# A preset of partial maxima moves from GpSimd to VectorE, in 27 of 32 units

## The chip, the cores and the metric

The kernel runs on one core of one Trainium2 chip. The metric is the time of one execution on the device, in microseconds (us); lower is better. Engines are named as the profile names them: PE is TensorE (PEld its weight loads), DVE is VectorE, ACT is ScalarE, POOL is GpSimd, SP is SyncE, which issues nearly all DMAs here.

## The reference

One transformer block over 2048 tokens of width 512: attention with 32 query heads of width 16 that share one key and one value head, then a gated MLP of width 1792, both behind a layer norm and a residual. All in float32.

```
q = (ln(x) @ wq) as 32 heads of 16;  k = ln(x) @ wk;  v = ln(x) @ wv
p = softmax((q @ k.T) * 16 ** -0.5)           # over all 2048 keys
h = x + concat(p @ v) @ wo
gate = ln(h) @ W_gate;  up = ln(h) @ W_up
out = h + (gate * (gate > 0) * up) @ W_down
```

## The kernel before

**Units.** Attention is done in 32 units. A unit is 256 tokens of 8 heads, that is 2048 query rows. Each unit passes twice over the keys. The first pass finds each query row's greatest score (letters `m` and `M` of the row of letters below, lower and upper half of PE's rows): a matmul of 128 query rows by 512 keys into one PSUM bank (line 655), and a `tensor_reduce` of DVE that leaves one number per row (line 665). The second pass (`e`, `E`) makes the scores again with keys on the partitions (line 702), ACT takes the exponential (line 705), and a value block (`O`, line 718) multiplies with v.

**The partial maxima.** A unit's numbers go to a tile `mpart`, `[128, 2, 2, 4, 4]`: half of PE's rows, part, block of 128 rows, and last the slot j, one for each 512 keys. When all are there, `max_finish` reduces over the four slots (line 670) and three more DVE operations and a DMA round trip bring the maximum into the queries of the second pass. Two tiles `mpart` take turns (`bufs=2`).

**Joint maxima.** In places the third and fourth blocks of keys are done together (letters `d`, `D`): PE multiplies with `kdiff`, the difference of the two blocks' keys; ACT makes its positive part (line 659); and DVE adds it to the fourth block's scores and takes the maximum in one operation (line 662, with an accumulator read behind it). The result stands in slot 3, and slot 2 is never written. So that line 670 can read it, the whole tile is set to -3e38 when the unit begins, by a POOL `memset` on line 651.

**What else POOL does.** The MLP's weights come by DMA as raw float32 (`wraw`) and are split into a rounded and a rest part, two POOL operations a tile (lines 246 and 247), the same for the hidden activations `hT`. For each of 14 hidden blocks f of a token tile POOL runs, in this order: the product `hf` (line 913), the split of two tiles `gu` (gate and up weights of f+2), of `hT`, and of `wd`. It also normalises the attention output (line 768: `raw` times `scale`, which come by DMA) and splits it. POOL works through its queue in order of the program.

**What sets the order.** A row of letters `ORDER` is written in the kernel; a loop takes a letter after another and emits that pass on PE at once, with what ACT and DVE do with its result. MLP passes are the letters `g`, `G` (line 304). Work of POOL and the DMAs is emitted when a simple model of the clocks of the engines (`on`, `at`, `due`) says so; the model has no entry for the memset. Each engine then runs its own instructions in the order of emission, and semaphores hold an instruction until its operands are ready and its buffer is free.

Of the kernel before, what the change touches and what calls it, by code (L numbers as in the profile page):

```python
# [26 lines left out]
STEPS = NB * 2  # L27
# [10 lines left out]
PASS, LOAD, SEEN, CHANGE, VALUE, BACK, TURN = 230, 107, 425, 95, 882, 237, 214  # L38

EXP, EXP_FREE, RED, RED_FREE, COPY, ADD, FREE = 494, 650, 600, 740, 541, 600, 150  # L40
JOINT, APART, RELUS = 640, 2900, 3
ROUND, DIFF, PRODUCT, SCALE, HOP, ISSUE = 640, 1290, 1150, 640, 2600, 600
APPLY, LANDING, ASKED, SPREAD, RAW_LAG = 705, 4700, 5500, 5600, 1500

# [113 lines left out]
def block_kernel(ctx: ExitStack, tc: tile.TileContext, x, wq, wkv, wo, wgu, wd, out):  # L158
    nc = tc.nc
# [37 lines left out]
    def bank(tag=None):  # L197
        if tag is None:
            tag = rota["tags"][rota["n"] % len(rota["tags"])]
            rota["n"] += 1  # L200
        return ps.tile([128, 512], F32, name=tag, bufs=1)
# [7 lines left out]
    def on(engine, t, ns):  # L209

        clk[engine] = max(clk[engine], t) + ns
        return clk[engine]
# [418 lines left out]
    mpart = {}  # L631

    def max_step(m):

        i = m % STEPS
        if i < STEPS // 2:
            return i // 8, i // 4 % 2, i % 4
        return 2 + i % 2, (i - STEPS // 2) // 8, (i - STEPS // 2) // 2 % 4
# [1 line left out]
    def key_of(m):  # L640
        return "key", max_step(m)[0]

    relus = {}

    def max_mm(m, ab, tag, apart=False):

        v = m // STEPS
        j, p, c = max_step(m)
        if v not in mpart:
            mpart[v] = sb.tile([128, 2, 2, 4, 4], F32, name="mpart", bufs=2)  # L650
            nc.gpsimd.memset(mpart[v], -3e38)
        r = slice(64 * ab, 64 * ab + 62)
        b = bank(tag)
        keys = kdiff[r] if apart else kaug[r, j * 512:(j + 1) * 512]
        nc.tensor.matmul(b, qaug[v][r, p, c * 128:(c + 1) * 128], keys, start=True, stop=True)  # L655
        part = mpart[v][:, ab, p, c, j:j + 1]
        if apart:
            relus[ab] = sb.tile([128, T], F32, name="relu", bufs=RELUS)
            nc.scalar.activation(relus[ab], b, AF.Relu)  # L659
        elif ab in relus:  # L660
            over = relus.pop(ab)
            nc.vector.tensor_tensor_reduce(out=over, in0=b, in1=over, scale=1.0, scalar=-3e38, op0=ALU.add, op1=ALU.max,  # L662
                                           accum_out=part)
        else:
            nc.vector.tensor_reduce(part, b, axis=AX.X, op=ALU.max)  # L665
# [552 lines left out]
    while not done():  # L1218
# [78 lines left out]
        letter = next(order)  # L1297
# [8 lines left out]
        kind, k = letter.upper(), int(letter.isupper())  # L1306
# [4 lines left out]
        if kind == "O":  # L1311
            value_block(on_)
            v, i = divmod(on_, NB)
# [12 lines left out]
        elif kind == "E":  # L1326
# [7 lines left out]
            ge[k] += 1  # L1334
        elif kind == "D":
            max_mm(me[k], k, tag, True)
            lanes[k] = s + PASS
            slots[k] = len(joined)
# [6 lines left out]
        elif kind == "M":  # L1345
            joint = k in relus
            max_mm(me[k], k, tag)
            lanes[k] = s + PASS
            r0 = max(clk["V"], s + SEEN, relu_end.pop(k, 0.0))
# [61 lines left out]
```

## Time and profile before

| | |
|---|---|
| median of 3 runs | 1771.95 us (1770.25 to 1772.96) |
| the profiled execution | 1770.07 us |
| its span, first to last instruction | 1768.3 us |
| mean granted TensorE clock | 0.981 |
| busy: PE, DVE, ACT, POOL | 1707.0, 1388.4, 1299.8, 844.4 us |

The profiled execution has 1.8 us around its span. In the answers quoted below, a row of the chain or the timeline reads: start, duration, engine, line, operation, out <- in, count, and in brackets how long the engine sat idle before it and what ended that. A row of the waits reads: who, on which line <- for whom: total us, times, longest. A row of a table of stretches gives the busy time of each engine with the number of its instructions, then the granted TensorE clock (1.00 is full speed), the DMAs' share and rate.

### The profile page before, as it was taken

How to read it: one execution, taken by the hardware profiler on the slowest of the kernel's cores; microseconds unless marked ns; L12 is line 12 of the kernel's file. 1: busy time of each engine (PE TensorE's matmuls, PEld its weight loads, DVE VectorE, ACT ScalarE, POOL GpSimd, SP SyncE). 2: the span in 40 equal slices, each digit the busy share in tenths (PEclk: the TensorE clock that was granted, in tenths of full speed). 3: DMA queues.
4: the chain of work that ended last, by engine and by line, in shares of the span. 5: the costliest groups of instructions: out<-in, count | busy, mean ns of one | idle time of the engine just before them, and what ended most of it. 6: DMA issues, size and time to landing. Idle time of an engine off the chain costs nothing.

```text
span 1768.3 us, 40468 instructions
## 1 busy us (share of the span) xinstructions
PE 1707.0 (97%) x15566; PEld 1153.7 (65%) x15566; DVE 1388.4 (79%) x2546; ACT 1299.8 (74%) x2628; POOL 844.4 (48%) x1034
## 2 busy tenths in 40 slices
PE   8999999889999999999899989999999999999999
PEld 6774345556666676676667667666656667666688
DVE  8698998768888887878688768877769888894355
ACT  6577998668778777877677767875667877778734
POOL 4624001545626456376635547276443766454510
PEclk9899999989999999999999999999999999999999
DMA  3233011221223222233213222222222222233333
GB/s 127 72 110 112 23 32 41 80 73 62 82 70 98 65 89 89 77 95 94 64 47 104 77 76 88 69 84 67 79 81 65 86 85 76 62 107 98 112 124 118
DMA packets 101972, 144.09 MB, mean 81 GB/s; under 512 B 27156, under 2 KB 39572, under 8 KB 101780
## 3 DMA queue, kind: packets, MB, share of 16 engines
q1 hardware_dynamic: 100724, 141.19, 25.9%
q8 instruction: 122, 2.00, 0.5%
q14 instruction: 70, 0.57, 0.1%
q10 hardware_dynamic: 1056, 0.33, 0.1%
HBM read 119.73 MB, written 21.49 MB: 80 GB/s over the span
## 4 chain that ended last, share of the span: by engine, by line
PE 77%; POOL 12%; issue 6%; DVE 2%; DMA 1%; ACT 1%; SPq 0%; POOLq 0%; ACTq 0%; DVEq 0%
PE B L304 24%; PE O L718 23%; PE B L702 15%; PE B L655 11%; POOL gu L247 4%; PE B L295 3%; POOL wd L247 2%; POOL gu L246 2%; DVE mpart L665 1%; POOL hT L247 1%; POOL hf L913 1%; POOL wd L246 1%; PE B L536 1%; POOL hT L246 1%; PE O L970 0%
## 5 line engine op out<-in xcount | busy, mean ns | idle before, releaser
L705 ACT ACTIVATE p<-B 128x512 f32<-128x512 f32 x2048 | 1067.8, 613 | 337.8 <-PE B L655 193.5
L665 DVE TENSOR_REDUCE mpart<-B 128x1 f32<-128x512 f32 x1760 | 1101.1, 683 | 251.1 <-PE B L655 150.0
L655 PE MATMUL B<-kaug,qaug 62*128 62x512 f32 x1904 | 714.7, 422 | 28.8 <-DVE mpart L665 23.9
L702 PE MATMUL B<-qaug,kaug 64*128 64x512 f32 x2048 | 712.0, 414 | 20.2 <-DVE mpart L665 19.4
L304 PE MATMUL B<-hn,gu 64*128 64x256 f32 x4704 | 569.2, 281 | 0.0
L304 PEld LDWEIGHTS B<-hn,gu 64*128 64x128 f32 x4704 | 545.0, 186 | 22.2 <-issue 15.4
L718 PE MATMUL O<-p,vv 128*32 128x512 f32 x4096 | 511.0, 607 | 0.0
L702 PEld LDWEIGHTS B<-qaug,kaug 64*128 64x128 f32 x2048 | 342.4, 186 | 217.8 <-DVE mpart L665 69.0
L655 PEld LDWEIGHTS B<-kaug,qaug 62*128 62x128 f32 x1904 | 333.8, 186 | 89.0 <-DVE mpart L665 37.4
L304 PE MATMUL B<-wd,hT 64*128 64x512 f32 x1176 | 295.4, 402 | 0.1
L913 POOL TENSOR_TENSOR hf<-hf,ga 128x256 f32<-128x256 f32 x88 | 64.6, 734 | 421.3 <-ACT hf L911 400.3
L247 POOL TENSOR_TENSOR gu<-wraw,gu 128x512 fp32r<-128x512 f32 x191 | 247.7, 1297 | 15.9
L718 PEld LDWEIGHTS O<-p,vv 128*32 128x32 f32 x4096 | 103.0, 109 | 213.4 <-issue 195.7
L304 PEld LDWEIGHTS B<-wd,hT 64*128 64x128 f32 x1176 | 196.9, 189 | 23.8 <-issue 10.2
L246 POOL TENSOR_SCALAR gu<-wraw 128x512 fp32r<-128x512 f32 x191 | 118.4, 620 | 25.3 <-PE B L304 24.8
L247 POOL TENSOR_TENSOR wd<-wraw,wd 128x512 fp32r<-128x512 f32 x90 | 115.8, 1287 | 7.5
L662 DVE CUSTOM_DVE_ANT_0 relu<-B,relu 128x512 f32<-128x512 f32 x144 | 96.7, 685 | 21.4 <-PE B L655 7.3
L768 POOL TENSOR_TENSOR raw<-raw,scale 128x512 f32<-128x512 f32 x15 | 19.3, 1287 | 192.3 <-DMA scale<-r_dram 126.0
L659 ACT ACTIVATE relu<-B 128x512 f32<-128x512 f32 x144 | 84.8, 605 | 23.9 <-PE B L655 23.2
L304 PE MATMUL B<-wo,act 64*128 64x512 f32 x384 | 88.5, 391 | 0.0
L247 POOL TENSOR_TENSOR hT<-hf,hT 128x256 fp32r<-128x256 f32 x97 | 74.1, 764 | 8.1
L905 ACT ACTIVATE ga<-B 128x256 f32<-128x256 f32 x112 | 44.1, 393 | 37.1 <-PE B L295 22.7
(156 smaller groups left out, 1112.2 us busy)
## 6 DMA issues: line engine op xcount, KB each, us to landing
wraw<-wgu SPq DMA_DIRECT2D x224, 256.0 KB
wraw<-wd SPq DMA_DIRECT2D x112, 256.0 KB
q_dram<-act SPq DMA_DIRECT2D x32, 256.0 KB
qaug<-q_dram SPq DMA_DIRECT2D x62, 128.0 KB
o_dram<-osb SPq DMA_DIRECT2D x31, 256.0 KB
x<-x SPq DMA_DIRECT2D x18, 256.0 KB
out<-h SPq DMA_DIRECT2D x16, 256.0 KB
qaug<-q_dram SPq DMA_DIRECT2D x62, 64.0 KB
```

The costliest lines, as they stand in the source:

```text
L246: nc.gpsimd.tensor_scalar(dst[:, 0], src, 1.0, 0.0, op0=ALU.mult, op1=ALU.add)
L247: nc.gpsimd.tensor_tensor(dst[:, 1], src, dst[:, 0].bitcast(F32), op=ALU.subtract)
L295: nc.tensor.matmul(out(self.bank), l(a), r(b), start=i == 0, stop=i == len(self.ops) - 1)
L304: mm = nc.tensor.matmul(out(self.bank), l(a)[rows], r(b)[rows], start=opens and which == 0, stop=closes and which == 1)
L655: nc.tensor.matmul(b, qaug[v][r, p, c * 128:(c + 1) * 128], keys, start=True, stop=True)
L659: nc.scalar.activation(relus[ab], b, AF.Relu)
L662: nc.vector.tensor_tensor_reduce(out=over, in0=b, in1=over, scale=1.0, scalar=-3e38, op0=ALU.add, op1=ALU.max, accum_out=part)
L665: nc.vector.tensor_reduce(part, b, axis=AX.X, op=ALU.max)
L702: nc.tensor.matmul(b, kaug[r, kb * 128:(kb + 1) * 128], qaug[v][r, p, :], start=True, stop=True)
L705: nc.scalar.activation(probs[g][:, ab], b, AF.Exp, scale=DH ** -0.5)
L718: nc.tensor.matmul(obank[v][32 * h:32 * h + 32], vv[:, kb, :], probs[g + p][:, ab], start=kb == 0, stop=kb == NB - 1)
L913: nc.gpsimd.tensor_tensor(hf[:, :n], hf[:, :n], ga[:, :n], op=ALU.mult)
```

## The change

The preset of a unit's whole `mpart` tile (64 numbers a partition) on POOL is gone. Ahead of the loop, the kernel counts through the row of letters which units have joint maxima: 27 of the 32. In these alone DVE presets slot 2, which is 16 numbers a partition, `memset` on what is line 658 of the changed kernel. In the other five units all four slots are written, and nothing is preset. `CLEAR` is the cost that the clock model takes for the DVE operation, and it is 0. The row of letters is the same, and the lines behind the change have numbers 8 higher.

```diff
-JOINT, APART, RELUS = 640, 2900, 3
+JOINT, APART, RELUS, CLEAR = 640, 2900, 3, 0
...
-    relus = {}
+    relus, joint_units, counts = {}, set(), [0, 0]
+    for letter in ORDER:
+        if letter in "mMdD":
+            k = int(letter.isupper())
+            if letter in "dD":
+                joint_units.add(counts[k] // STEPS)
+            counts[k] += 1
...
     def max_mm(m, ab, tag, apart=False):
...
             mpart[v] = sb.tile([128, 2, 2, 4, 4], F32, name="mpart", bufs=2)
-            nc.gpsimd.memset(mpart[v], -3e38)
+            if v in joint_units:
+                nc.vector.memset(mpart[v][:, :, :, :, 2:3], -3e38)
+                on("V", 0.0, CLEAR)
```

Leaving out the presets, the order of instructions on PE, DVE, ACT, POOL and SP is the same in both kernels. Two places show the move, both at the begin of the eighth unit (342 us in the trace). First POOL's queue in the kernel before; `hf` is the product of one hidden block, `gu`, `hT` and `wd` are the tiles that POOL splits behind it:

```order
L913 TENSOR_TENSOR hf_4648<-hf_4648,ga_4647 128x256
L246 TENSOR_SCALAR gu_4652<-wraw_4492 128x512
L247 TENSOR_TENSOR gu_4652<-wraw_4492,gu_4652 128x512
L246 TENSOR_SCALAR gu_4655<-wraw_4494 128x512
L247 TENSOR_TENSOR gu_4655<-wraw_4494,gu_4655 128x512
L246 TENSOR_SCALAR hT_4378<-hf_4648 128x256
L247 TENSOR_TENSOR hT_4378<-hf_4648,hT_4378 128x256
L246 TENSOR_SCALAR wd_4660<-wraw_4382 128x512
L247 TENSOR_TENSOR wd_4660<-wraw_4382,wd_4660 128x512
L651 MEMSET mpart_4673 128x64
L913 TENSOR_TENSOR hf_4803<-hf_4803,ga_4802 128x256
```

The memset of the new unit's `mpart` stands behind a hidden block's nine operations, the first of which needs ACT's result; in the changed kernel POOL goes from `wd` to the next `hf`.

Second DVE's queue at the same place, in the kernel before (`ISA` rows are the joint maxima of line 662 and their accumulator reads; `mpart_4045` is the unit that is ending, `mpart_4673` the one that begins):

```order
L662 ISA relu_4579,mpart_4045<-B4_4638,relu_4579 128x512
L662 ISA mpart_4045 128x1
L662 ISA relu_4633,mpart_4045<-B5_4666,relu_4633 128x512
L662 ISA mpart_4045 128x1
L665 TENSOR_REDUCE mpart_4673<-B0_4675 128x1
L665 TENSOR_REDUCE mpart_4673<-B4_4691 128x1
L665 TENSOR_REDUCE mpart_4673<-B3_4694 128x1
```

And in the changed kernel (the tiles' running numbers are 3 lower):

```order
L670 ISA relu_4576,mpart_4042<-B4_4635,relu_4576 128x512
L670 ISA mpart_4042 128x1
L670 ISA relu_4630,mpart_4042<-B5_4663,relu_4630 128x512
L670 ISA mpart_4042 128x1
L658 MEMSET mpart_4670 128x16
L673 TENSOR_REDUCE mpart_4670<-B0_4672 128x1
L673 TENSOR_REDUCE mpart_4670<-B4_4688 128x1
L673 TENSOR_REDUCE mpart_4670<-B3_4691 128x1
```

The preset now stands on DVE right ahead of the unit's first reduce, which before was on another engine than its preset and waited for a semaphore of POOL's besides the one of PE's; of the reduces only the first of a unit did so.

## The prediction

> **What bounds the kernel now.** I read the page's busy times first, then the waits by engine, then the preset's own line, then the timeline and a table of stretches at the places that these named.
>
> ```profile
> PE 1707.0 (97%) x15566; PEld 1153.7 (65%) x15566; DVE 1388.4 (79%) x2546; ACT 1299.8 (74%) x2628; POOL 844.4 (48%) x1034
> ...
> DVE mpart L665 <- POOL mpart L651: 49.8, 10, 8.6
> ...
> PE B L655 <- DVE mpart L665: 23.9, 7, 7.1
> PE B L702 <- DVE mpart L665: 19.4, 4, 7.0
> ...
> L651 POOL MEMSET mpart<- x32: 141/152/161, 25.2 to 1543.3; 128x64 f32 x32
> ```
>
> PE is the bound: it idles 1768.3 - 1707.0 = 61 us in all, and in 23.9 + 19.4 = 43.3 us of them it waited for a reduce of DVE. DVE in turn waited 49.8 us for the memset, which itself lasts 0.15 us. The timeline shows how so short an operation costs so much:
>
> ```profile
> 334.33 0.73 POOL L913 TENSOR_TENSOR hf<-hf,ga 128x256 f32<-128x256 f32 x1 [0.89 <-ACT hf L911]
> 334.54 0.08 DVE L662 DVE_READ_ACCUMULATOR2_ANT mpart<- 128x1 f32 x1
> 335.50 0.39 PE L655 MATMUL B<-kaug,qaug 62*128 62x512 f32 x1
> 341.97 0.15 POOL L651 MEMSET mpart<- 128x64 f32 x1
> 342.15 1.89 DVE L665 TENSOR_REDUCE mpart<-B 128x1 f32<-128x512 f32 x3 [7.53 <-POOL mpart L651]
> 342.90 0.79 PE L702 MATMUL B<-qaug,kaug 64*128 64x512 f32 x1 [7.01 <-DVE mpart L665]
> ```
>
> The memset stood in POOL's queue behind a hidden block (hf, gu, hT, wd) that POOL began at 334.33 and that took 7.6 us. DVE stops at 334.6 at the new unit's first reduce, the banks fill, PE stops at 335.9. All go on when the memset is done: DVE 0.03 us after it, PE 0.75 us later, after one reduce. So a head-of-line wait on POOL stops the bound, at 342 us for 7.01 us. Seven more places have it:
>
> ```profile
> 160.59 1.29 DVE L665 TENSOR_REDUCE mpart<-B 128x1 f32<-128x512 f32 x2 [2.98 <-POOL mpart L651]
> 388.67 0.69 DVE L665 TENSOR_REDUCE mpart<-B 128x1 f32<-128x512 f32 x1 [7.83 <-POOL mpart L651]
> 884.51 1.29 DVE L665 TENSOR_REDUCE mpart<-B 128x1 f32<-128x512 f32 x2 [8.49 <-POOL mpart L651]
> 1041.55 1.89 DVE L665 TENSOR_REDUCE mpart<-B 128x1 f32<-128x512 f32 x3 [8.55 <-POOL mpart L651]
> 1195.97 2.73 DVE L665 TENSOR_REDUCE mpart<-B 128x1 f32<-128x512 f32 x4 [4.31 <-POOL mpart L651]
> 1250.06 1.29 DVE L665 TENSOR_REDUCE mpart<-B 128x1 f32<-128x512 f32 x2 [3.76 <-POOL mpart L651]
> 1305.95 1.29 DVE L665 TENSOR_REDUCE mpart<-B 128x1 f32<-128x512 f32 x2 [5.14 <-POOL mpart L651]
> ```
>
> The eight are 48.6 of the 49.8 us. The next table is the one on which the sum rests. Each of its first eight stretches runs from PE's stop to the end of the low clock that follows:
>
> ```profile
> 159.67:165.85 6.18, 4.51 (x21) 1.48 (x25) 4.58 (x9) 2.97 (x6) 0.89 (x2) 0.72 0.09 23
> 335.89:346.75 10.86, 3.85 (x17) 1.65 (x19) 2.93 (x6) 1.59 (x4) 5.98 (x8) 0.69 0.18 48
> 382.31:394.54 12.23, 5.12 (x27) 1.28 (x26) 3.26 (x7) 0.63 (x2) 6.08 (x8) 0.58 0.17 49
> 878.58:889.47 10.89, 4.22 (x21) 4.12 (x22) 4.03 (x7) 2.42 (x5) 5.64 (x8) 0.69 0.05 14
> 1036.16:1046.49 10.33, 4.20 (x20) 3.73 (x21) 4.56 (x11) 2.39 (x4) 5.10 (x8) 0.67 0.03 5
> 1191.51:1200.09 8.58, 3.38 (x16) 2.03 (x19) 3.96 (x8) 1.26 (x3) 4.26 (x6) 0.80 0.01 2
> 1247.51:1254.70 7.19, 3.90 (x21) 1.57 (x24) 4.38 (x8) 0.70 (x2) 2.43 (x4) 0.76 0.08 17
> 1302.33:1312.73 10.40, 6.03 (x31) 2.47 (x34) 4.71 (x11) 2.08 (x5) 3.42 (x6) 0.67 0.14 38
> sum 76.66, PE 35.22 PEld 18.34 DVE 32.41 ACT 14.04 POOL 33.80; mean PE 4.40 PEld 2.29 DVE 4.05 ACT 1.75 POOL 4.23
> ...
> 339.93:346.75 6.82, 3.85 (x17) 1.65 (x19) 2.93 (x6) 0.94 (x2) 2.10 (x4) 0.50 0.13 38
> 400.00:860.00 460.00, 459.90 (x4482) 311.75 (x4480) 383.78 (x706) 359.80 (x730) 263.57 (x322) 1.00 0.26 80
> ```
>
> Length less PE's busy time is the idle time: 76.66 - 35.22 = 41.4 us. But the stop costs more than its idle time. From 339.93 to 346.75 the granted clock is 0.50, and PE worked 3.85 us of it, all after the stop. All eight stretches contain such a spell (their mean clock is 0.58 to 0.80), and in 460 us without a stop the clock is 1.00. In that long stretch an instruction of PE's takes 460 / 4482 = 0.1026 us; the eight hold 174 instructions, which at that pace take 17.9 us, not 35.2.
>
> **The rule on the clock.** The Trainium skill, "TensorE: Matmul & The Clock Gate", Part 1, says that TensorE falls to half clock after an idle window of about 3.4 us and comes back after as much work. The six stops of 4.4 us and more agree; the ones of 1.67 us (first row) and 3.29 us (seventh) are followed by half clock too, which is sooner than the rule. By that page's price, half of the throttled time is lost: some 17 of the 35.2 us on top of the idle time, an estimate by which the kernel would come out 3 us faster than by my sum.
>
> **The removed memset.** What do the eight stretches take without the wait? At least PE's time at full clock, the count by 0.1026 us. And at least DVE's, which works at its own clock, less the lead that DVE has because it stopped earlier than PE: its wait, less PE's idle time, plus the 0.75 us between their restarts. Row by row (lead; DVE's work less lead; PE's time):
> - 2.06; 2.52; 2.15
> - 1.27; 1.66; 1.74
> - 1.47; 1.79; 2.77
> - 2.57; 1.46; 2.15
> - 3.17; 1.39; 2.05
> - -0.14; 4.10; 1.64
> - 1.22; 3.16; 2.15
> - 1.52; 3.19; 3.18
>
> The greater of the last two, summed, is 21.7 us, so 76.7 - 21.7 = 55.0 us come back. The two smaller DVE waits (49.8 - 48.6 = 1.2 us) I count as 0.8, since PE has 43.3 - 41.4 = 1.9 us of idle time for DVE elsewhere. Sum: 55.8. Ends: 41.4 if only the idle time returned, and 76.7 - 17.9 + 1.2 = 60.0 if PE alone set the pace. I stand nearer the upper, since both engines' work is counted. POOL's own 32 x 0.15 = 4.8 us count nothing: POOL is busy 48% of the time and waits elsewhere.
>
> **The new memset on DVE.** 27 instructions on 16 numbers a partition. The rows nearest are
>
> ```profile
> L187 DVE MEMSET vv<- 128x16 f32 x1 | 0.1, 72 | 0.1
> L674 DVE CAST msplit<-mfin x32: 174/175/1297, 85.7 to 1597.2; 128x16 fp32r<-128x16 f32 x32
> L674 DVE CAST msplit<-mfin 128x16 fp32r<-128x16 f32 x32 | 10.9, 341 | 1.1
> ```
>
> The first has the operation and the size: 27 x 0.072 = 1.9 us. The cast has the size and is held at times (0.175 us in the median, 1.297 at most); priced like its mean, 27 x 0.341 = 9.2 us. The lower end is 0, where DVE was idle at a unit's begin anyway. A gain is excluded, as DVE only gets work. I take 1.9 and put all of it on the path, because DVE is what PE waits for at these places. It waits for no other engine's tile: the one that read the buffer last is DVE itself (line 670), earlier in its queue. Behind it on DVE stands the unit's first reduce, and behind that PE's banks.
>
> The Trainium skill, "SBUF — State Buffer", section "Who interferes with whom", says that a cast can take the port pair that DVE shares with GpSimd, and that a DVE instruction with at most one SBUF input outside the two-port modes doesn't contend. By it the memset isn't held and the sum is that of 0.072; the spread of the cast agrees with the page's first half, and no row shows a memset beside a busy POOL.
>
> **What is late next.** In the stop POOL and the DMAs went on while PE did not; now PE comes up to 9 us earlier to the same place. POOL then had time to spare: its idle time up to its next operation covers the shift unless it is shorter. The shortest are
>
> ```profile
> 350.94 0.74 POOL L913 TENSOR_TENSOR hf<-hf,ga 128x256 f32<-128x256 f32 x1 [8.82 <-ACT hf L911]
> 892.31 1.28 POOL L768 TENSOR_TENSOR raw<-raw,scale 128x512 f32<-128x512 f32 x1 [7.83 <-DMA scale<-r_dram]
> 1209.84 1.29 POOL L768 TENSOR_TENSOR raw<-raw,scale 128x512 f32<-128x512 f32 x1 [13.90 <-DMA scale<-r_dram]
> 1315.09 1.29 POOL L768 TENSOR_TENSOR raw<-raw,scale 128x512 f32<-128x512 f32 x1 [9.17 <-DMA scale<-r_dram]
> ...
> 1200.66 0.24 DVE L752 RECIPROCAL sums<-sums 128x16 f32<-128x16 f32 x1
> ```
>
> The shifts there are 10.86 - 1.74 = 9.1, 10.89 - 2.15 = 8.7, 8.58 - 4.10 = 4.5 and 10.40 - 3.19 = 7.2 us, so POOL comes 0.3 and 0.9 us too late at the first two. I count 1.2 us. At the other two the DMAs bring the reciprocals of line 752, which stood on DVE behind the stopped reduce (at 1200.66 in one case) and so move with it.
>
> **Sum.** 55.8 - 1.9 - 1.2 = 52.7 us. The profiled execution, 1770.07 us, becomes 1717.4; against the median of 1771.95 that is 1719 us, 3.0% less. About 0.2%, 3.5 us, is what a measurement can tell from no change.
>
> **Rivals.**
> - *Only the idle time returns*: DVE and ACT, freed of their rest, set the pace where PE had crawled. 1771.95 - 41.4 - 0.8 + 3.1 = 1733. For it, DVE is busy 79%; against it, its work in the stretches is counted above. Chance 0.12.
> - *POOL becomes the wait*: PE comes to the weights before POOL has split them. The block that begins at 334.33 runs to 342 whatever DVE does. The last three stretches, where raw or a late DMA stands first in POOL's queue, would lose their 4.5 + 4.0 + 7.2 = 15.7 us: 1735. Against it, the idle times above, and no row of the waits of PE names gu or wd. Chance 0.10.
> - *The wait was another's*: the semaphore named came last only by chance, and PE stays stopped. Then 1774. Against it, DVE restarts within 0.03 us of the memset's end. Chance 0.02.
> - *Slower: the new memset is held on DVE.* It stands ahead of every reduce of its unit, so a hold stops PE as the old one did. To eat 55 us each of the 27 must be held 2.0 us; the longest hold of a like operation is the cast's 1.297 us, and even that every time leaves 1771.95 - 55.8 + 35 = 1751. Over 1776 only with holds beyond any row. Chance 0.02.
>
> My forecast (1713 to 1727) has 0.71; the last 0.03 is for other ends, such as a new stop elsewhere. The range goes from 1711 (upper end 60.0, next to nothing paid) to 1734, which takes in the first rival and part of the second. Faster by over 0.2%: 0.95; within: 0.03; slower: 0.02.
>
> **What would show it.** Right: DVE's waits have no row for POOL at mpart; PE's waits for line 665's successor (673) fall from 43 to a few us; no spell of 0.50 between 160 and 1700 us; memsets of DVE at some 70 ns; mean clock from 0.981 to 0.99 or more; PE's instruction count unchanged. Wrong: PE or PEld waiting for gu or wd for several us, spells of 0.50 that remain, memsets of several hundred ns, or DVE's waits for ACT or PE grown at the unit begins.

## The result, and the profile after

The changed kernel takes 1713.66 us (median of 4 runs, 1712.52 to 1715.31) where the kernel before takes 1772.45 on the same chip: 58.8 us less, a ratio of 0.967 with a 95% interval of 0.9653 to 0.9686. The forecast was 1719 (1711 to 1734). The profiled execution has a span of 1710.8 us against 1768.3, which is 57.5 us less, and a mean clock of 0.993 against 0.981.

The busy times on the page, and of the chain of waits the shares by engine (before, PE had 77% of that chain and POOL 12%):

```profile
PE 1691.1 (99%) x15566; PEld 1148.1 (67%) x15566; DVE 1388.6 (81%) x2573; ACT 1298.6 (76%) x2628; POOL 841.6 (49%) x1002
...
PE 95%; DVE 2%; POOL 1%; issue 1%; DMA 0%; ACT 0%; POOLq 0%; SPq 0%; DVEq 0%; ACTq 0%
```

PE has the same 15566 instructions. Its idle time fell from 61.3 us to 1710.8 - 1691.1 = 19.7, by 41.6 us, and its busy time from 1707.0 to 1691.1, by 15.9 us. The two make up the 57.5 us: the first is the stops, the second is low clock, since the same instructions took less time.

The waits by engine, PE's on DVE and DVE's longest:

```profile
PE B L710 <- DVE mpart L673: 1.1, 2, 0.8
PE B L663 <- DVE mpart L673: 0.2, 1, 0.2
...
DVE mpart L673 <- PE B L663: 144.8, 159, 3.8
```

PE's 43.3 us of waits for the reduces are 1.3 us, and DVE's waits have no row for the preset. The preset's own line, and the timeline of DVE, POOL and ACT at the place that stood at 342 us before:

```profile
L658 DVE MEMSET mpart<- x27: 72/72/72, 26.2 to 1498.6; 128x16 f32 x27
...
333.07 0.08 DVE L670 DVE_READ_ACCUMULATOR2_ANT mpart<- 128x1 f32 x1
333.10 0.67 DVE L673 TENSOR_REDUCE mpart<-B 128x1 f32<-128x512 f32 x1
333.12 0.07 DVE L658 MEMSET mpart<- 128x16 f32 x1
334.03 1.29 DVE L673 TENSOR_REDUCE mpart<-B 128x1 f32<-128x512 f32 x2 [0.26 <-PE B L663]
...
339.40 1.29 POOL L247 TENSOR_TENSOR wd<-wraw,wd 128x512 fp32r<-128x512 f32 x1
340.00 0.38 ACT L919 ACTIVATE hf<-B 128x256 f32<-128x256 f32 x1
340.64 0.74 POOL L921 TENSOR_TENSOR hf<-hf,ga 128x256 f32<-128x256 f32 x1
```

In DVE's queue the memset stands ahead of the unit's first reduce, which is the one at 333.10; the record of the memset begins 0.02 us behind that of the reduce and ends inside it. Ahead of the second reduce DVE is idle for 0.26 us, because of a matmul; before, it was idle for 7.53 us ahead of the first. POOL splits the same block as before, until 340.7, and PE does not wait for it. POOL has no idle time left ahead of the next `hf`: ACT's part of it ends at 340.38 and POOL takes it up at 340.64, 0.3 us late.

The eight stretches of the prediction, found again in the changed kernel by their matmuls (the n-th of each kind), and taken from the start of the last matmul ahead of the stop to the first matmul that starts behind the low clock. Before, these took 6.6, 11.4, 13.1, 11.4, 10.9, 9.1, 7.8 and 11.1 us, 81.4 in all:

```profile
161.75:164.66 2.91, 2.91 (x24) 0.99 (x24) 2.36 (x5) 2.33 (x5) 1.57 (x2) 1.00 0.11 24
334.03:336.15 2.12, 2.12 (x20) 0.91 (x18) 2.12 (x5) 1.71 (x4) 2.03 (x3) 1.00 0.02 9
...
1152.42:1155.78 3.36, 2.56 (x18) 1.16 (x19) 3.33 (x8) 1.65 (x3) 3.19 (x5) 1.00 0.10 30
1202.80:1205.36 2.56, 2.56 (x24) 1.22 (x24) 2.56 (x6) 1.10 (x3) 2.39 (x4) 1.00 0.03 10
...
sum 22.60, PE 21.80 PEld 11.26 DVE 20.84 ACT 14.10 POOL 20.34; mean PE 2.72 PEld 1.41 DVE 2.61 ACT 1.76 POOL 2.54
```

All have clock 1.00, and 81.4 - 22.6 = 58.8 us came back.

### The profile page after: what moved, and what is told of

Same layout as the page of the kernel before. It is cut to its first block, busy times and chain, and to the rows that moved or that the text cites. A ratio compares the mean times of both kernels' runs of the same rounds, so it can differ in the third digit from the quotient of the medians.

```text
span 1710.8 us, 40447 instructions
## 1 busy us (share of the span) xinstructions
PE 1691.1 (99%) x15566; PEld 1148.1 (67%) x15566; DVE 1388.6 (81%) x2573; ACT 1298.6 (76%) x2628; POOL 841.6 (49%) x1002
## 4 chain that ended last, share of the span: by engine, by line
PE 95%; DVE 2%; POOL 1%; issue 1%; DMA 0%; ACT 0%; POOLq 0%; SPq 0%; DVEq 0%; ACTq 0%
PE B L304 29%; PE O L726 28%; PE B L710 18%; PE B L663 14%; PE B L295 4%; DVE mpart L673 1%; PE B L536 1%; PE O L978 0%; PE B L411 0%; POOL kaug L517 0%; PE B L603 0%; DVE kaug L517 0%; PE B L1053 0%; DVE msplit L682 0%; DMA qaug<-c_dram 0%
## 5 line engine op out<-in xcount | busy, mean ns | idle before, releaser
L304 PEld LDWEIGHTS B<-hn,gu 64*128 64x128 f32 x4704 | 544.2, 186 | 22.5 <-issue 15.4
L726 PE MATMUL O<-p,vv 128*32 128x512 f32 x4096 | 504.1, 600 | 0.0
L663 PEld LDWEIGHTS B<-kaug,qaug 62*128 62x128 f32 x1904 | 332.1, 185 | 62.1 <-ACT p L713 18.4
L304 PE MATMUL B<-wd,hT 64*128 64x512 f32 x1176 | 288.7, 395 | 0.1
L247 POOL TENSOR_TENSOR gu<-wraw,gu 128x512 fp32r<-128x512 f32 x191 | 247.9, 1298 | 15.9
L304 PEld LDWEIGHTS B<-wd,hT 64*128 64x128 f32 x1176 | 193.3, 185 | 23.7 <-issue 10.2
```

The source lines that it names most:

```text
L247: nc.gpsimd.tensor_tensor(dst[:, 1], src, dst[:, 0].bitcast(F32), op=ALU.subtract)
L304: mm = nc.tensor.matmul(out(self.bank), l(a)[rows], r(b)[rows], start=opens and which == 0, stop=closes and which == 1)
L726: nc.tensor.matmul(obank[v][32 * h:32 * h + 32], vv[:, kb, :], probs[g + p][:, ab], start=kb == 0, stop=kb == NB - 1)
```

## The experiments

Two questions were open behind a result that agreed: which part of the change takes the stops away, since it does three things at once (another engine, a smaller region, fewer units); and which terms of the sum were off by 6 us. All ran beside runs of the kernel before, whose medians lie between 1772.2 and 1772.6 us; times are medians. The edits are shown against the changed kernel, that of part 1 against the kernel before.

**The base.** The changed kernel again, on the chip of three of the kernels below: the one with the preset earlier on POOL, the one with eight memsets for one, and the one with none.

> The changed kernel once more, as the base on this chip for the three beside it. Every theory: 1713.7 us, give or take 1.5, some 58.8 us under the kernel before.

1714.72 us, ratio 0.9674 (0.9658 to 0.9689).

**Part 1: the place in POOL's queue.** The preset stays on POOL, whole tile, all units, and is emitted earlier.

```diff
+    def preset(v):
+        mpart[v] = sb.tile([128, 2, 2, 4, 4], F32, name="mpart", bufs=2)
+        nc.gpsimd.memset(mpart[v], -3e38)
...
         if v not in mpart:
-            mpart[v] = sb.tile([128, 2, 2, 4, 4], F32, name="mpart", bufs=2)
-            nc.gpsimd.memset(mpart[v], -3e38)
+            preset(v)
...
     def max_finish(v):
...
         at(t + HOP, landed)
+        if v + 2 < len(UNITS):
+            at(t, lambda: v + 2 in mpart or preset(v + 2))
```

> The preset stays on POOL, whole tiles in all 32 units, but is emitted when the tile's last reader (two units back) has finished, about one unit ahead of its use. Theory (the place in POOL's queue made the stops): the stops go as with VectorE, 1713 to 1717 us, no low clock between 160 and 1700 us, and DVE waits under 3 us for the memset in all. Rival (the engine matters: a semaphore from POOL or POOL's work at the unit begins costs the time wherever the memset stands): it stays above 1750 us.

1715.15 us, ratio 0.9677 (0.966 to 0.9694): the same as the changed kernel. DVE's waits have no row for the memset. The wait for a free tile went to POOL, where it costs nothing (waits of POOL):

```profile
POOL mpart L648 <- DVE mfin L674: 85.5, 12, 44.7
```

So for a preset of the whole tile it was the place. POOL may preset the tile, even wait 44.7 us for it, if nobody is behind it at that moment. One spell of low clock stands between 160 and 1700 us against the expectation, at 1648 us. The changed kernel that ran beside it has one at 1646 (in both the mean clock from 1600 to 1700 us is 0.98), so it is not this preset's.

**Part 2: the smaller region and fewer units, on POOL.**

```diff
             if v in joint_units:
-                nc.vector.memset(mpart[v][:, :, :, :, 2:3], -3e38)
-                on("V", 0.0, CLEAR)
+                nc.gpsimd.memset(mpart[v][:, :, :, :, 2:3], -3e38)
```

> One part of the change alone: the preset of slot 2 in the 27 joint units, on POOL as before; the five other units have none. Theory (the place in POOL's queue makes the stops): only the stop at 160 us goes, which is that of a unit without joint maxima, so 3 to 4 us under the kernel before, about 1768.5. Rival (the preset of 64 numbers or its number of instructions matters): more than 10 us under it.

1713.78 us, ratio 0.9671 (0.9656 to 0.9685). My expectation, 1768.5, missed by 55 us: here the memset stands in POOL's queue exactly where it stood before, behind the same blocks, and no stop is left. DVE's waits for POOL, all of them:

```profile
DVE hf L915 <- POOL gu L247: 11.2, 2, 6.5
DVE hf L915 <- POOL gu L246: 3.5, 1, 3.5
DVE xn L385 <- POOL rs L364: 0.8, 1, 0.8
```

None is for the preset. In the program, a unit's first reduce writes slot 0. The whole preset writes it too, so that reduce had to wait for POOL; a preset of slot 2 alone concerns only reduces into slot 2 and the final one. The timeline shows it at the begin of the eighth unit, whose first reduce is the one at 335.67:

```profile
335.67 0.69 DVE L672 TENSOR_REDUCE mpart<-B 128x1 f32<-128x512 f32 x1
336.62 1.29 DVE L672 TENSOR_REDUCE mpart<-B 128x1 f32<-128x512 f32 x2 [0.27 <-PE B L662]
...
343.26 0.14 POOL L658 MEMSET mpart<- 128x16 f32 x1
```

The reduces run while POOL is still 7.6 us away from the memset of their tile. The next reduce that has a wait for POOL's semaphore starts at 374.99, when the memset is long done.

**Part 3: fewer units alone**, the whole tile on POOL in 27 units, to tell the region from the five dropped presets.

```diff
             if v in joint_units:
-                nc.vector.memset(mpart[v][:, :, :, :, 2:3], -3e38)
-                on("V", 0.0, CLEAR)
+                nc.gpsimd.memset(mpart[v], -3e38)
```

> The preset on POOL in the 27 joint units alone, but of the whole tile, where the kernel with the preset of slot 2 alone on POOL came out at 1713.8 us. Theory (what holds DVE is that the preset writes slot 0, which the unit's first reduce writes too; a preset of slot 2 alone holds only a reduce into slot 2, dozens of DVE's instructions later): the stops come back at seven places, all but that at 160 us, 1767 to 1770 us. Rival (dropping the preset in the five other units shifted POOL's queue enough): within 5 us of 1713.8.

1769.1 us, ratio 0.9979 (0.9969 to 0.9988). The stops are back, all but that at 160 us:

```profile
DVE mpart L672 <- POOL mpart L658: 46.7, 8, 8.6
```

So in part 2 it was the region, not the count.

**Part 4: the engine alone**, whole tile on DVE in all 32 units.

```diff
-            if v in joint_units:
-                nc.vector.memset(mpart[v][:, :, :, :, 2:3], -3e38)
-                on("V", 0.0, CLEAR)
+            nc.vector.memset(mpart[v], -3e38)
```

> The other part of the change alone: the preset moves to VectorE, of the whole tile and in all 32 units (128x64, some 0.112 us each by the two that another kernel ran at its start). Theory (either part by itself takes the stops away, and VectorE hides 0.1 us at a unit's begin): 1713 to 1717 us. Rival (only with the narrow preset do the stops go): above 1760. If VectorE hides nothing: 32 x 0.112 - 27 x 0.072 = 1.6 us over the changed kernel, 1716.

1719.58 us, ratio 0.9685 (0.9662 to 0.9707), runs from 1713.35 to 1721.03. No stops: moving the preset is enough for that too. But the median lies 2.6 us above the 1717 that I gave as the upper end and 5.9 above the changed kernel. The runs spread widely and the intervals of the two overlap; the traces say more. Matched matmul by matmul with the changed kernel's, this kernel's lie 3.3 us later at 200 us and 7.4 later at 1600, so it lost 4.1 us over 28 presets. The three kernels without a preset on DVE (those of parts 1 and 2, and the last one below) lost 0.8 to 1.2 us in the same stretch, so about 1 us is what this comparison can tell. DVE at the begin of the eighth unit:

```profile
336.86 0.09 DVE L668 DVE_READ_ACCUMULATOR2_ANT mpart<- 128x1 f32 x1
336.91 0.11 DVE L657 MEMSET mpart<- 128x64 f32 x1
337.12 1.97 DVE L671 TENSOR_REDUCE mpart<-B 128x1 f32<-128x512 f32 x3
```

The first reduce starts 0.26 us behind the accumulator read, where in the changed kernel it is 0.02 (333.07 and 333.10). The whole preset writes slot 0, so the reduce has to wait for it on DVE too; its record has a wait for DVE's own semaphore. So the narrow region is worth some 3 to 4 us on this engine.

**The memset's price.** Eight memsets for one, and none.

```diff
             if v in joint_units:
-                nc.vector.memset(mpart[v][:, :, :, :, 2:3], -3e38)
-                on("V", 0.0, CLEAR)
+                for _ in range(8):
+                    nc.vector.memset(mpart[v][:, :, :, :, 2:3], -3e38)
```

> Each of the 27 presets on VectorE is done eight times instead of once: 189 more memsets of 0.072 us, 13.6 us more work for DVE. Theory of the prediction (DVE's added time at the unit begins lies on PE's path): 13 to 14 us over the changed kernel, about 1727. Rival (DVE has slack at most unit begins, so that the 1.9 us of the prediction were not paid): under 5 us over it, below 1719.

1737.24 us, ratio 0.9802 (0.9788 to 0.9817): 22.5 us over the base, more than the 13.6 of either theory. The group of its memsets shows why:

```profile
L659 DVE MEMSET mpart<- 128x16 f32 x216 | 15.6, 72 | 13.3
```

Memsets of the same tile in a row wait for each other by DVE's own semaphore, 13.3 us in all, or 0.07 us ahead of each further one. So DVE got 189 x 0.142 = 26.8 us more, and 22.5 us, 84%, reached the end: at a unit's begin DVE is on the path once it is held for about 1 us.

Then the kernel with no preset; slot 2 of a joint maximum keeps what an earlier unit left in it.

```diff
+    maxima = [consts.tile([128, 2, 2, 4, 4], F32, name=f"mpart{i}") for i in range(2)]
...
+    for m in maxima:
+        nc.vector.memset(m, -3e38)
...
-            mpart[v] = sb.tile([128, 2, 2, 4, 4], F32, name="mpart", bufs=2)
-            if v in joint_units:
-                nc.vector.memset(mpart[v][:, :, :, :, 2:3], -3e38)
-                on("V", 0.0, CLEAR)
+            mpart[v] = maxima[v % 2]
```

> No unit has a preset: two fixed tiles are set once at the start and take turns, so slot 2 of a joint maximum holds what an earlier unit left there (that part of the result is changed; the time is not). It takes the 27 memsets off DVE. Theory of the prediction (all 1.9 us on the path): 1.9 us under the changed kernel, about 1711.8. Rival (hidden): within 0.7 us of it.

1713.32 us, ratio 0.9664 (0.9648 to 0.9681): 1.4 us under the base with intervals that overlap, which can't tell 0 from 1.9. The traces can, a little: matched matmul by matmul with the changed kernel's, this kernel's lie 1.3 us earlier at 200 us (all of it from the start, up to 100 us), 0.8 at 400, 1.0 at 1150 and 0.1 at 1600. So without the 25 presets between 200 and 1600 us it gained nothing. Alone, a memset is nearly hidden: in the median a reduce starts together with the accumulator read ahead of it, and at the three places where a memset stands between the two, 0.024 to 0.037 us after it. That would make 27 x 0.037 = 1.0 us at most, an estimate.

**The price of a stop.** The changed kernel with DVE held at the begin of the eight units that had stops, by 6 memsets of 128x512 (the short hold, shown here) or 17 (the long one).

```diff
+    hold = consts.tile([128, 512], F32, name="hold")
...
                 on("V", 0.0, CLEAR)
+            if v in (3, 7, 8, 18, 21, 24, 25, 26):
+                for _ in range(6):
+                    nc.vector.memset(hold, 0.0)
```

> The changed kernel, with DVE held at the begin of the eight units that had a stop: six memsets of a spare tile (128x512, about 0.49 us each, 2.9 us) ahead of the first reduce. In the kernel before a DVE wait was 0.9 us longer than PE's stop, so PE should stop about 2 us at each place: 8 x 2.0 = 16 us idle. Theory 1 (any stop of PE brings low clock behind it, as the stop of 1.67 us did in the kernel before): 2 us more at each place, 32 us over the changed kernel, about 1746. Theory 2 (a stop must be longer than some 3 us): no low clock, 16 us over it, about 1730.

1751.82 us, ratio 0.988 (0.986 to 0.9899), 38 us over the changed kernel.

> As the kernel with the short hold, with 17 memsets in place of six, 8.2 us at each of the eight places. PE should stop 7.3 us: 8 x 7.3 = 58 us idle. Theory (low clock follows each stop, and costs half of the 3.4 to 6 us that it lasts): eight spells of clock 0.50, some 17 us more, 75 us over the changed kernel, about 1789. Rival (the low clock costs nothing because DVE and ACT catch up in it): 58 us over it, about 1772.

1810.49 us, ratio 1.0213 (1.019 to 1.0235), 97 us over it. The busy times of the two, the short one first:

```profile
PE 1706.5 (98%) x15566; PEld 1150.1 (66%) x15566; DVE 1411.2 (81%) x2621; ACT 1299.3 (74%) x2628; POOL 843.6 (48%) x1002
```

```profile
PE 1709.9 (94%) x15566; PEld 1156.0 (64%) x15566; DVE 1454.6 (80%) x2709; ACT 1299.6 (72%) x2628; POOL 843.3 (47%) x1002
```

With spans of 1748.5 and 1809.4 us PE idled 42.0 and 99.5 us, 22.3 and 79.8 more than in the changed kernel, and was busy 15.4 and 18.8 us longer with the same instructions. Both came out above what I expected because the memsets of one tile wait for each other here too (6.9 and 22.2 us in all), which made the holds longer than I had counted. The price beside the idle time is what was expected of the long hold: 18.8 us for eight stops of 8.5 to 11.8 us, some 2.3 us each. So low clock is not free, and the rival of that is out. Nearly all of the 18.8 is low clock: in the long hold's spells of clock 0.50 PE worked 36.7 us, of which half is 18.4. In the short hold it worked 22.9 us in them, of which half is 11.4; the other 4 us of the 15.4 are not explained. The short holds stopped PE for 1.3 to 4.6 us. The six stops of 2.08 us and more are followed by low clock, those of 1.87 and 1.29 are not, so neither of the two theories holds. Two of the eight on the timeline of PE, and for each the stretch in which the stop begins and the one behind it:

```profile
165.95 0.54 PE L667 MATMUL B<-kaug,qaug 62*128 62x512 f32 x1 [2.08 <-DVE mpart L677]
876.76 0.50 PE L714 MATMUL B<-qaug,kaug 64*128 64x512 f32 x1 [1.87 <-DVE mpart L677]
...
162.86:166.28 3.42, 1.34 (x9) 0.59 (x6) 2.87 (x6) 1.08 (x2) 1.53 (x2) 1.00 0.07 27
166.28:169.69 3.41, 3.41 (x15) 1.03 (x14) 2.22 (x6) 0.69 (x2) 0.00 (x0) 0.50 0.09 17
872.84:876.26 3.42, 2.04 (x19) 0.48 (x11) 2.55 (x7) 1.10 (x3) 3.20 (x4) 1.00 0.16 62
876.26:879.67 3.41, 2.91 (x23) 2.17 (x25) 3.41 (x7) 2.06 (x4) 3.20 (x5) 1.00 0.11 11
```

The stretches are not chosen freely. In each trace the granted clock changes only at whole multiples of 3.413 us from its first change: in the kernel before the spells begin at 162.43, 339.93, 384.30 us and so on, 52 and 13 such periods apart, and last one, two or three of them. The stop of 2.08 us lies within one period, that of 1.87 us in two, with 1.4 us in the first. I counted PE's idle time by these periods in all traces, from 100 to 1600 us. Of the periods that began at full clock, the 28 with 1.99 us or more of idle time were all followed by half clock, and none with 1.4 or less was; of six with 1.55 to 1.75, two were. So two stops of nearly the same length can differ: that of 1.87 us here and one of 1.88 in the kernel with eight memsets, of which 1.55 lie in one period and which has half clock behind it. Idle time alone is not the whole rule: the spell at 1648 us follows a period with only 0.8 us of it.

## Why the prediction was right, and where not

**The mechanism held.** The stops were those of a reduce behind a memset behind a block of POOL's work: with the wait gone, PE's idle time fell by 41.6 us where the stretches had 41.4. The low clock went with them, 15.9 us of PE's busy time, so the rival in which only the idle time returns is out, and the long hold shows the same price from the other side. POOL did not become the wait, and the memset was not held on DVE: 72 ns each, minimum and maximum.

**What I took for one cause was two.** The prediction put the stops to the preset's being on POOL. Each of three edits takes them away by itself: another engine (1719.58), an earlier place (1715.15), or a region that the first reduce doesn't write (1713.78). For the stops it makes no difference which; as an account of the change it was incomplete, since the narrow region alone would have done it. On DVE the region still counts: the whole tile there lost some 4 us, since the unit's first reduce waits for it.

**The sum was 6 us too small** (52.7 against 58.8 of the medians). By its terms:
- *What the eight stretches take without the wait* was mis-sized: 21.7 us by the greater of PE's and DVE's time, so 55.0 back. 58.8 came back, which in the sum is PE's time alone (76.7 - 17.9 = 58.8). Of the 3.8 us between them, 2.5 lie at the sixth and seventh, where I had let DVE set the pace with 4.10 and 3.16 us: 5.8 and 5.2 us came back there where my rows gave 4.5 and 4.0. DVE was on the path only at the sixth, as its stretch of 3.36 us with 3.33 of DVE and 2.56 of PE shows; in the others PE is busy throughout. Why my rows gave DVE too much there was not shown; I had counted all reduces that DVE did in the low clock as work that belongs between the stretch's matmuls. The other 1.3 us are spread over the remaining rows, and that the sum meets PE's time alone is luck, as the sixth stayed 1.2 us short of it.
- *The memset*, 1.9 us, is near nothing: without the presets no time was gained that the traces can tell. I put all of it on the path because DVE is waited for there. That is right for 1 us a unit and wrong for 0.07, of which only 0.02 to 0.04 delays the reduce behind it.
- *POOL late*, 1.2 us, was not paid. At the first of the two places POOL is late by the 0.3 us that I forecast (340.64 against 340.38), but the waits of PE have no row for `gu`, `wd` or `hT` of POOL, and those of its weight loads have 1.7 us for `hT` as before, so nothing of it reached PE.
- *The start* went against it: up to 100 us the changed kernel is 3.0 us behind by the matched matmuls, with a lower clock (0.87, the second row below) than the kernel before (0.91, the first row). The kernel without presets has 0.91 there and those of parts 1 and 2 have 0.87, so it differs from trace to trace and is not shown to be the change's. I had no term for it, and what sets the clock there was not studied. From 100 to 1600 us the changed kernel gained 60.3 us, about the 60.0 that I gave for the upper end.

```profile
5.00:100.00 95.00, 83.79 (x544) 67.49 (x543) 71.19 (x144) 59.37 (x116) 48.27 (x57) 0.91 0.32 99
```

```profile
5.00:100.00 95.00, 83.39 (x515) 66.89 (x515) 68.06 (x141) 56.75 (x112) 46.63 (x54) 0.87 0.31 96
```

**The rule on the clock.** The Trainium skill, "TensorE: Matmul & The Clock Gate", Part 1, puts the fall to half clock behind an idle window of about 3.4 us. The runs differ: 2.08 us sufficed in the short hold, and 1.67 us in the kernel before; what agrees is the length of the window, as the clock changes here in steps of 3.41 us. Its price, half of the throttled time, fits: in the spells of the kernel before PE worked 33.6 us, half of which is 16.8, and its busy time fell by 15.9 over the whole kernel, with the slower start in it. By that price I named an end 3 us faster than my sum; that the time came out 5 us faster does not confirm it, since the terms above make up that difference.

## What to carry to other kernels

A short operation on an idle-looking engine can stop TensorE if it stands behind that engine's long work and ahead of the bound's: look who waits for it, not how long it lasts. Before moving it, ask which part of its output the first waiter touches; a narrower write, an earlier emission or the waiter's own engine each cut the same wait here, the last with 3 to 4 us left to pay until the write was narrowed too. And price a stop of TensorE, in a kernel like this one, at its idle time plus about 2 us of low clock behind it, if it lasts more than some 2 us; a stop of 1.5 us can cost it too.

## What the runs showed of the hardware that I had not expected

- The granted clock of TensorE changes only on a fixed grid of 3.413 us, and what precedes half clock is idle time within one such period: always with 1.99 us or more of it, two times in six with 1.55 to 1.75, never with 1.4 or less (100 to 1600 us, all traces). So stops of 1.67 us (kernel before) and 1.88 us (eight memsets) had half clock behind them, and one of 1.87 us in the short hold, which fell into two periods, had none.
- A 128x16 memset of VectorE between an accumulator read and a reduce that doesn't touch what it wrote delays the reduce by 0.024 to 0.037 us, though it lasts 0.072. Where the next operation writes the same numbers, it waits: memsets in a row cost 0.142 us each, and the reduce behind a 128x64 memset started 0.26 us after the read in place of 0.02.
